# SwiGLU feed-forward on one core: the first 256 tokens turned on TensorE instead of in their load

## The chip, the cores and the metric

The kernel runs on one core of a Trainium2 chip. The metric is device microseconds of one execution. Durations of single instructions come from one profiled execution of each kernel.

## The reference

```python
B, S, D, F = 1, 2048, 512, 1376          # all bfloat16
def reference(x, w_gate, w_up, w_down):
    g = silu(x @ w_gate)                 # (2048, 1376)
    u = x @ w_up
    return (g * u) @ w_down              # (2048, 512)
```

## The kernel before

TensorE needs the contracted dimension on the 128 partitions. So the kernel holds x transposed: `xT_sb` has 128 partitions, four blocks of 128 features (`KD` = 4) and 2048 tokens. The tokens are worked in four chunks of 512 (`SC`), the 1376 columns of the two weights in ten blocks of 128 plus a rest of 96.

For a chunk `c` and a column block `ft` there are two groups of four matmuls: a gate group G and an up group U. Each group adds up over the four feature blocks into one of eight PSUM banks; the banks are taken in turn (`add_group`, group number modulo 8), and a group waits for the readers of the group eight places earlier. ScalarE takes silu of a G bank into `sg_sb` (L214), VectorE multiplies that with the U bank into `hT_sb` (L221). The rests of 96 columns are done in X groups (L283) and Y groups (L294). After all four chunks come sixteen O groups of eleven matmuls each (L311), which multiply `hT_sb` with w_down; VectorE copies their banks to `o_sb` (L225) and SyncE stores them (L197). The order on every engine is written out by hand; nothing is scheduled by a program.

The loads, on which the beginning depends, are issued from two queues.

- ScalarE's queue issues the first column block of w_gate and of w_up (`wg0`, `wu0`, 128 KB each), and only then loads its activation table and runs a small dummy activation (L203).
- SyncE's queue issues everything else, in this order: `x0a`, tokens 0 to 255, and `x0b`, tokens 256 to 511, by transposing loads (L73); then the weight slabs, always gate before up (L78): `wg1`, `wu1` (column block 1), `wg2`, `wu2` (blocks 2 and 3), `wg4`, `wu4` (4 to 6), `wg7`, `wu7` (7 to the end), the 32 last columns `wut`; then `x1`, `x2`, `x3` by transposing loads of 512 tokens each; then w_down.

TensorE first runs `N_WARM` = 10 matmuls on constants of one (L267), whose results nobody reads. Then the first pair of groups is worked in two halves of 256 tokens, so that it can begin when only `x0a` is there:

```python
for n0, n1 in ((0, HT), (HT, SC)):
    for g in groups[0:2]:
        gu_matmuls(g, n0, n1)
```

`gu_matmuls` waits once for each load that it is the first to need: `x0a` and `wg0`, then `wu0`, then `x0b` for the second halves, then `wg1`, `wu1`, `wg2`, `wu2` and so on. All later groups follow one after the other. GpSimd writes four small constants at the start (L334), and has nothing else to do.

Of the kernel before, what the change touches and what calls it, by code (L numbers as in the profile page):

```python
# [5 lines left out]
ALU = mybir.AluOpType  # L6
BF16 = mybir.dt.bfloat16
FP32 = mybir.dt.float32

N_WARM = 10  # L10


def bass_standalone__swiglu_ffn__prompt_kernel(nc, x, w_gate, w_up, w_down, out):
    _, S, D = x.shape
    F = w_gate.shape[1]
    P = 128
# [6 lines left out]
    TPC = SC // P  # L23
    NST = S // P
    LASTA = 384
    HT = SC // 2
# [5 lines left out]
    xf = x[0]  # L32
# [8 lines left out]
    with ExitStack() as es:  # L41
        sb = lambda name, shape, dt: es.enter_context(nc.sbuf_tensor(name, shape, dt))
        ps = lambda name, shape, dt: es.enter_context(nc.psum_tensor(name, shape, dt))
        sem = lambda name: es.enter_context(nc.semaphore(name))

        xT_sb = sb("xT_sb", [P, KD, S], BF16)
# [4 lines left out]
        sg_sb = [sb(f"sg_sb{i}", [P, SC], FP32) for i in range(NSG)]  # L51
        sgx_sb = [sb(f"sgx_sb{c}", [P, SC], FP32) for c in range(NSC)]
        sgy_sb = [sb(f"sgy_sb{c}", [P, SC], FP32) for c in range(NSC)]
        o_sb = [sb(f"o_sb{i}", [P, D], BF16) for i in range(NOS)]
        banks = [ps(f"bank{i}", [P, 512], FP32) for i in range(NB)]

        s_P = sem("s_P")
        s_A = sem("s_A")
        s_D = sem("s_D")
        s_out = [sem(f"s_out{i}") for i in range(NOS)]  # L60
        loads = {}

        def load_sem(name):
            loads[name] = sem(f"s_{name}")
            return loads[name]
# [6 lines left out]
        def load_x(eng, name, t0, t1):  # L72
            eng.dma_start_transpose(  # L73
                xT_sb[:, :, t0:t1], xf[t0:t1, :]
            ).then_inc(load_sem(name), 16)

        def load_w(eng, name, src, base, f0, f1):
            eng.dma_start(  # L78
                w_sb[:, :, base + f0:base + f1],
                src[:, f0:f1].rearrange("(k p) f -> p k f", p=P),  # L80
            ).then_inc(load_sem(name), 16)
# [1 line left out]
        slabs = [(0, 1), (1, 2), (2, 4), (4, 7), (7, NFT)]  # L83
        slab_of = {ft: a for a, b in slabs for ft in range(a, b)}

        def load_slab(eng, a, b):
            load_w(eng, f"wg{a}", w_gate, 0, a * P, min(b * P, F))
            load_w(eng, f"wu{a}", w_up, UPH, a * P, min(b * P, F - 32))

        def loads_on_scalar(act):  # L90
            load_slab(act, *slabs[0])

        def loads_on_sync(sp):
            load_x(sp, "x0a", 0, HT)
            load_x(sp, "x0b", HT, SC)
            for a, b in slabs[1:]:
                load_slab(sp, a, b)
            load_w(sp, "wut", w_up, F - (F - 32), F - 32, F)
            for c in range(1, NSC):
                load_x(sp, f"x{c}", c * SC, (c + 1) * SC)  # L100
            sp.dma_start(
                wd_sb[:, 0:NFF, :], w_down[0:NFF * P, :].rearrange("(k p) d -> p k d", p=P)
            ).then_inc(load_sem("wd"), 16)
            sp.dma_start(wd_sb[0:F_LAST, NFF, :], w_down[NFF * P:F, :]).then_inc(load_sem("wdt"), 16)
# [7 lines left out]
        def add_group(kind, **what):  # L112
            g = dict(kind=kind, at=len(groups), bank=banks[len(groups) % NB], readers=[], **what)
            groups.append(g)
            return g

        def add_op(eng, g, **what):
            n_read[eng] += 1
            op = dict(g=g, at=n_read[eng], **what)
            (act_ops if eng == "A" else dve_ops).append(op)  # L120
            g["readers"].append((eng, op["at"]))
            return op
# [37 lines left out]
        def plan_y(pi):  # L160
            g = add_group("Y", pi=pi)
            for c in (2 * pi, 2 * pi + 1):
                y0, y1 = yblk(c)
                d = add_op(
                    "D", g, kind="mul", out=hT_sb[0:64, NFF, c * SC:(c + 1) * SC],
                    a=sgy_sb[c][y0:y1, :], b=g["bank"][y0:y1, :], after=y_after[c],
                )
                t_ready[c] = d["at"]

        for c in range(NSC):  # L170
            for ft in range(NFF):
# [21 lines left out]
        def on_sync(sp):  # L193
            loads_on_sync(sp)
            for t, c0, c1, ob, eng, n in stores:
                sp.wait_ge(s_A if eng == "A" else s_D, n)
                sp.dma_start(of[t * P:(t + 1) * P, c0:c1], o_sb[ob][:, c0:c1]).then_inc(s_out[ob], 16)  # L197
            for i in range(NOS):
                sp.wait_ge(s_out[i], 16 * n_store[i])
# [28 lines left out]
        def on_tensor(pe):  # L228
            landed = set()

            def need(name):
                if name not in landed:
                    pe.wait_ge(loads[name], 16)
                    landed.add(name)

            read = {"A": 0, "D": 0}

            def after(eng, n):
                if n > read[eng]:
                    pe.wait_ge(s_A if eng == "A" else s_D, n)  # L240
                    read[eng] = n

            def free(g):
                if g["at"] >= NB:
                    for eng, n in groups[g["at"] - NB]["readers"]:
                        after(eng, n)

            def gu_matmuls(g, n0, n1):
                c, ft = g["c"], g["ft"]
                if c > 0:  # L250
                    need(f"x{c}")
                elif n0 < HT:
                    need("x0a")
                if c == 0 and n1 > HT:
                    need("x0b")
                need(("wg" if g["kind"] == "G" else "wu") + str(slab_of[ft]))
                col = (0 if g["kind"] == "G" else UPH) + ft * P
                for dk in range(KD):
                    ins = pe.matmul(  # L259
                        g["bank"][:, n0:n1], lhsT=w_sb[:, dk, col:col + P],  # L260
                        rhs=xT_sb[:, dk, c * SC + n0:c * SC + n1], start=(dk == 0), stop=(dk == KD - 1),
                    )
                if n1 == SC:
                    ins.then_inc(s_P, 1)

            for i in range(N_WARM):
                pe.matmul(banks[NB - 1][:, :], lhsT=ones_w, rhs=ones_m, start=True, stop=True)  # L267

            for n0, n1 in ((0, HT), (HT, SC)):
                for g in groups[0:2]:  # L270
                    gu_matmuls(g, n0, n1)

            for g in groups[2:]:
                free(g)
                kind = g["kind"]
                if kind in "GU":
                    gu_matmuls(g, 0, SC)
                elif kind == "X":
                    c = g["c"]
                    need(f"wg{slab_of[NFF]}")  # L280
                    need("wut")
                    for dk in range(KD):
                        ins = pe.matmul(  # L283
                            g["bank"][:, :], lhsT=w_sb[:, dk, XC0:XC0 + P],
                            rhs=xT_sb[:, dk, c * SC:(c + 1) * SC],
                            start=(dk == 0), stop=(dk == KD - 1),
                        )
                    ins.then_inc(s_P, 1)
                elif kind == "Y":
                    need(f"wu{slab_of[NFF]}")  # L290
                    for dk in range(KD):
                        for c in (2 * g["pi"], 2 * g["pi"] + 1):
                            y0, y1 = yblk(c)
                            ins = pe.matmul(  # L294
                                g["bank"][y0:y1, :], lhsT=w_sb[:, dk, YC0:YC0 + 64],
                                rhs=xT_sb[:, dk, c * SC:(c + 1) * SC],
                                start=(dk == 0), stop=(dk == KD - 1),
                                tile_position=(0, y0), skip_group_check=True,
                            )
                    ins.then_inc(s_P, 1)  # L300
                else:
                    t, c0, c1 = g["t"], g["c0"], g["c1"]
                    c = t // TPC
                    need("wd")
                    after("D", h_ready[c])
                    for fk in range(NFT):
                        K = P if fk < NFF else F_LAST
                        if fk == NFF:
                            need("wdt")
                            after("D", t_ready[c])  # L310
                        ins = pe.matmul(  # L311
                            g["bank"][:, 0:c1 - c0], lhsT=hT_sb[0:K, fk, t * P:(t + 1) * P],
                            rhs=wd_sb[0:K, fk, c0:c1], start=(fk == 0), stop=(fk == NFT - 1),
                        )
                    ins.then_inc(s_P, 1)

        on_sync(nc.sync)
        on_scalar(nc.scalar)
        on_tensor(nc.tensor)
# [29 lines left out]
```

## Time and profile before

| | |
|---|---|
| time, median of 3 runs | 121.25 us (121.11 to 121.77) |
| the profiled execution's own time | 121.6 us |
| its span, first to last instruction | 120.3 us |
| PE busy | 116.4 us, 97% of the span |
| VectorE, ScalarE, GpSimd busy | 43.7, 30.3 and 0.2 us |
| granted TensorE clock | 1.000 |

The span is the time from the first to the last instruction; 1.3 us of the profiled execution lie around it. PE stands for TensorE's matmuls, PEld for its weight loads, which run beside them. SPq and ACTq are the queues on which SyncE and ScalarE issue transfers. Times with two decimals in the views count from the start of the span.

### The profile page before, as it was taken

What the parts mean: (1) busy time and instruction counts of PE and PEld (TensorE: products, weight loads), DVE (VectorE), ACT (ScalarE), POOL (GpSimd) and SP (SyncE); (2) the same over time, 40 slices, a digit from 0 to 9 for tenths busy, and PEclk for the clock granted to TensorE, in tenths of its full rate; (3) what the DMA queues carried; (4) which work ended last, traced back from release to release, by engine and by line L of the source; (5) the groups of instructions that cost most, each with busy time, mean ns of one, the idle gap of its engine ahead of it and who ended that gap; (6) DMA issues with size and microseconds to landing.
All of it is one profiled execution on the core that took longest, in us unless ns stands there. A gap on an engine that the chain in (4) does not pass through costs nothing.

```text
span 120.3 us, 1386 instructions
## 1 busy us (share of the span) xinstructions
PE 116.4 (97%) x547; PEld 53.4 (44%) x557; DVE 43.7 (36%) x64; ACT 30.3 (25%) x51; POOL 0.2 (0%) x4
## 2 busy tenths in 40 slices
PE   7899999999999999999999999999999999999993
PEld 2354444444444444444444444444444444444452
DVE  0024434444334444334444334466233223222420
ACT  4032333262333272333262332330000000000001
POOL 0000000000000000000000000000000000000000
DMA  3999999970000000000000000000211121112112
GB/s 83 224 281 373 241 253 138 260 257 0 0 0 0 0 0 5 0 0 3 3 0 0 0 5 0 0 0 0 87 44 44 48 87 45 44 63 67 44 44 87
DMA packets 18022, 8.51 MB, mean 71 GB/s; under 512 B 11520, under 2 KB 18016, under 8 KB 18016
## 3 DMA queue, kind: packets, MB, share of 16 engines
q1 hardware_dynamic: 16960, 8.16, 26.7%
q10 hardware_dynamic: 1056, 0.26, 1.0%
q8 instruction: 4, 0.07, 0.2%
q14 instruction: 2, 0.02, 0.1%
HBM read 4.23 MB, written 2.10 MB: 53 GB/s over the span
## 4 chain that ended last, share of the span: by engine, by line
PE 90%; DMA 4%; SPq 3%; issue 1%; DVE 0%
PE bank L259 54%; PE bank L311 32%; DMA w_sb<-in_w_gate_dram 4%; PE bank L283 3%; SPq L73 2%; PE bank L294 2%; SPq L78 1%; DVE o_sb L225 0%
## 5 line engine op out<-in xcount | busy, mean ns | idle before, releaser
L259 PE MATMUL bank<-xT_sb,w_sb 128*128 128x512 bf16 (+1 forms) x322 | 69.4, 374 | 0.9 <-DMA xT_sb<-in_x_dram 0.4
L259 PEld LDWEIGHTS bank<-xT_sb,w_sb 128*128 128x128 bf16 x328 | 31.9, 98 | 38.2 <-DMA xT_sb<-in_x_dram 0.9
L221 DVE TENSOR_TENSOR hT_sb<-sg_sb,bank 128x512 bf16<-128x512 f32 x40 | 27.5, 688 | 46.0 <-PE bank L259 38.1
L311 PE MATMUL bank<-wd_sb,hT_sb 128*128 128x512 bf16 (+4 forms) x184 | 38.1, 367 | 0.2
L214 ACT ACTIVATE sg_sb<-bank 128x512 f32<-128x512 f32 x40 | 23.8, 596 | 43.4 <-PE bank L259 43.4
L311 PEld LDWEIGHTS bank<-wd_sb,hT_sb 128*128 128x128 bf16 (+1 forms) x187 | 17.8, 98 | 20.7 <-DVE hT_sb L221 0.4
L225 DVE CAST o_sb<-bank 128x512 bf16<-128x512 f32 (+1 forms) x16 | 10.7, 667 | 25.4 <-PE bank L311 25.3
L214 ACT ACTIVATE o_sb<-bank 128x384 bf16<-128x384 f32 x1 | 0.5, 490 | 38.2 <-PE bank L311 38.2
L267 PE MATMUL bank<-const-bfloat16-1.0 128*128 128x512 bf16 x10 | 4.0, 582 | 0.8 <-PEq L334 0.8
L283 PE MATMUL bank<-xT_sb,w_sb 128*128 128x512 bf16 x15 | 4.1, 380 | 0.1
L221 DVE TENSOR_TENSOR hT_sb<-sgx_sb,bank 32x512 bf16<-32x512 f32 x4 | 2.8, 692 | 3.5 <-ACT sgx_sb L214 3.5
L214 ACT ACTIVATE sgx_sb<-bank 32x512 f32<-32x512 f32 x4 | 2.3, 587 | 4.5 <-PE bank L283 4.5
L221 DVE TENSOR_TENSOR hT_sb<-sgy_sb,bank 64x512 bf16<-64x512 f32 x4 | 2.7, 684 | 0.1
L267 PEld LDWEIGHTS bank<-const-bfloat16-1.0 128*128 128x128 bf16 x10 | 1.3, 139 | 3.0 <-issue 3.0
L283 PEld LDWEIGHTS bank<-xT_sb,w_sb 128*128 128x128 bf16 x16 | 1.6, 98 | 1.9
L214 ACT ACTIVATE sgy_sb<-bank 64x512 f32<-64x512 f32 x4 | 2.4, 589 | 0.1
L294 PE MATMUL bank<-xT_sb,w_sb 128*64 128x512 bf16 x16 | 1.9, 383 | 0.0
L203 ACT ACT_TABLE_LOAD x1 | 1.3, 1283 | 1.7 <-issue 1.7
L294 PEld LDWEIGHTS bank<-xT_sb,w_sb 128*64 128x64 bf16 x16 | 0.8, 110 | 1.0 <-DVE hT_sb L221 0.4
L203 ACT ACTIVATE act_dummy<-const-float32-0.0 128x4 f32<-128x4 f32 x1 | 0.2, 206 | 0.0
L334 POOL MEMSET const-bfloat16-1.0<- 128x1 bf16 x1 | 0.1, 101 | 0.0
L334 POOL MEMSET const-uint8-127<- 128x1 uint8 x1 | 0.1, 101 | 0.0
(2 smaller groups left out, 0.2 us busy)
## 6 DMA issues: line engine op xcount, KB each, us to landing
out_dram<-o_sb SPq DMA_DIRECT2D x15, 128.0 KB, 1.7
wd_sb<-in_w_down_dram SPq DMA_DIRECT2D x1, 1280.0 KB, 6.7
w_sb<-in_w_gate_dram SPq DMA_DIRECT2D x1, 480.0 KB, 6.5
w_sb<-in_w_up_dram SPq DMA_DIRECT2D x1, 448.0 KB, 6.9
w_sb<-in_w_gate_dram SPq DMA_DIRECT2D x1, 384.0 KB, 5.2
w_sb<-in_w_up_dram SPq DMA_DIRECT2D x1, 384.0 KB, 5.7
w_sb<-in_w_gate_dram SPq DMA_DIRECT2D x1, 256.0 KB, 4.4
w_sb<-in_w_up_dram SPq DMA_DIRECT2D x1, 256.0 KB, 4.7
```

The lines of the kernel that those rows point to most:

```text
L73: eng.dma_start_transpose(xT_sb[:, :, t0:t1], xf[t0:t1, :]).then_inc(load_sem(name), 16)
L78: eng.dma_start(w_sb[:, :, base + f0:base + f1], src[:, f0:f1].rearrange("(k p) f -> p k f", p=P),).then_inc(load_sem(name), 16)
L203: act.activation(adummy[:, 0:4], zero_c, ACT.Silu)
L214: act.activation(op["out"], op["src"], fn).then_inc(s_A, 1)
L221: ins = dve.tensor_tensor(op["out"], op["a"], op["b"], ALU.mult)
L225: ins = dve.tensor_copy(op["out"], op["src"])
L259: ins = pe.matmul(g["bank"][:, n0:n1], lhsT=w_sb[:, dk, col:col + P], rhs=xT_sb[:, dk, c * SC + n0:c * SC + n1], start=(dk == 0), stop=(dk ...
L267: pe.matmul(banks[NB - 1][:, :], lhsT=ones_w, rhs=ones_m, start=True, stop=True)
L283: ins = pe.matmul(g["bank"][:, :], lhsT=w_sb[:, dk, XC0:XC0 + P], rhs=xT_sb[:, dk, c * SC:(c + 1) * SC], start=(dk == 0), stop=(dk == KD - 1),
L294: ins = pe.matmul(g["bank"][y0:y1, :], lhsT=w_sb[:, dk, YC0:YC0 + 64], rhs=xT_sb[:, dk, c * SC:(c + 1) * SC], start=(dk == 0), stop=(dk == ...
L311: ins = pe.matmul(g["bank"][:, 0:c1 - c0], lhsT=hT_sb[0:K, fk, t * P:(t + 1) * P], rhs=wd_sb[0:K, fk, c0:c1], start=(fk == 0), stop=(fk == ...
L334: nc = _bacc.Bacc("TRN2", target_bir_lowering=False, num_devices=1)
```

## The change

Tokens 0 to 255 are no longer brought by a transposing load. Two plain loads `t0` and `t1` bring 128 tokens each, with the tokens on the partitions, into a new tile `x0_sb`. GpSimd writes a 128x128 identity `ident`. TensorE multiplies each of the eight 128x128 blocks with it, which turns the block; the results stand in four new groups T (two blocks each) in banks 0 to 3. ScalarE copies the first and third of them, VectorE the second and fourth, to the places in `xT_sb` that `x0a` filled. The first G group waits in front of its first matmul for ScalarE's copies and in front of its third for VectorE's. The dummies go from ten to six. `x0b` and all other loads stay, in the same order, and all groups from G on move on by four banks.

```diff
-N_WARM = 10
+N_WARM = 6
...
+        x0_sb = sb("x0_sb", [P, TPC // 2, D], BF16)
+        ident = sb("ident", [P, P], BF16)
...
+        s_I = sem("s_I")
...
         def loads_on_sync(sp):
-            load_x(sp, "x0a", 0, HT)
+            for t in range(TPC // 2):
+                sp.dma_start(x0_sb[:, t, :], xf[t * P:(t + 1) * P, :]).then_inc(load_sem(f"t{t}"), 16)
             load_x(sp, "x0b", HT, SC)
...
+        x0_ready = []
+        for t in range(TPC // 2):
+            for half, eng in enumerate("AD"):
+                g = add_group("T", t=t, k0=2 * half)
+                op = add_op(
+                    eng, g, kind="copy", stored=(s_I, 0),
+                    out=xT_sb[:, 2 * half:2 * half + 2, t * P:(t + 1) * P],
+                    src=g["bank"][:, 0:2 * P].rearrange("p (k t) -> p k t", k=2),
+                )
+                x0_ready.append((2 * half, eng, op["at"]))
+        n_T = len(groups)
...
-                elif n0 < HT:
-                    need("x0a")
-                if c == 0 and n1 > HT:
+                elif n1 > HT:
                     need("x0b")
...
                 for dk in range(KD):
+                    if c == 0 and n0 < HT:
+                        for k0, eng, n in x0_ready:
+                            if k0 <= dk:
+                                after(eng, n)
...
+            pe.wait_ge(s_I, 1)
+            for g in groups[:n_T]:
+                need(f"t{g['t']}")
+                for i in range(2):
+                    k = g["k0"] + i
+                    ins = pe.matmul(
+                        g["bank"][:, i * P:(i + 1) * P], lhsT=x0_sb[:, g["t"], k * P:(k + 1) * P],
+                        rhs=ident[:, :], start=True, stop=True,
+                    )
+                ins.then_inc(s_P, 1)
...
+        nc.gpsimd.affine_select(
+            ident[:, :], ones_w, pattern=[[-1, P]], compare_op=ALU.is_equal, fill=0.0, base=0,
+            channel_multiplier=1,
+        ).then_inc(s_I, 1)
         on_sync(nc.sync)
```

Compiled, the changed program has one more instruction that the diff does not show: on GpSimd, directly ahead of the select, stands one that reloads the engine's library of routines by its index (index 0). GpSimd's program before holds no such instruction.

## The prediction

> **What bounds the kernel now.** I read the page first: which engine is full, and on which lines the last chain lies.
>
> ```profile
> span 120.3 us, 1386 instructions
> PE 116.4 (97%) x547; PEld 53.4 (44%) x557; DVE 43.7 (36%) x64; ACT 30.3 (25%) x51; POOL 0.2 (0%) x4
> PE bank L259 54%; PE bank L311 32%; DMA w_sb<-in_w_gate_dram 4%; PE bank L283 3%; SPq L73 2%; PE bank L294 2%; SPq L78 1%; DVE o_sb L225 0%
> ```
>
> TensorE is full. Only the 7% on DMA and SPq lie outside its work, so a change at the start moves the time by as much as it moves the last of the early waits. The chain of waits in order of time shows which one that is:
>
> ```profile
> 0.73 1.33 SPq L73
> ...
> 2.11 1.29 SPq L73
> ...
> 3.46 0.58 SPq L78
> ...
> 4.62 4.44 DMA w_sb<-in_w_gate_dram
> ...
> 9.11 3.41 PE bank L259 x15
> ```
>
> The chain does not go through x0a's landing. It goes through SyncE's issues, x0a and x0b at 1.3 us each, to the third slab's gate half, wg2, which is issued at 4.62 and lands at 9.06. From 9.11 on matmul follows matmul. The timeline shows the same start from TensorE's side (two windows; the short rows are single dummies):
>
> ```profile
> 0.77 4.02 PE L267 MATMUL bank<-const-bfloat16-1.0 128*128 128x512 bf16 x10 [0.77 <-PEq L334]
> 1.73 1.28 ACT L203 ACT_TABLE_LOAD   x1 [1.73 <-issue]
> 5.20 3.65 PE L259 MATMUL bank<-xT_sb,w_sb 128*128 128x256 bf16 x24 [0.41 <-DMA xT_sb<-in_x_dram]
> 9.11 13.99 PE L259 MATMUL bank<-xT_sb,w_sb 128*128 128x512 bf16 x63 [0.26 <-DMA w_sb<-in_w_gate_dram]
> 3.71 0.63 PE L267 MATMUL bank<-const-bfloat16-1.0 128*128 128x512 bf16 x1
> 4.41 0.38 PE L267 MATMUL bank<-const-bfloat16-1.0 128*128 128x512 bf16 x1
> ```
>
> Full-width matmuls follow each other at 13.99 / 64 = 0.22 us (one of 64 records is missing), the dummies at about 0.43: half speed. Only the last dummy is short (0.38), so full speed came near 4.3 us, 3.5 us after the first dummy; the granted clock says 1.00 all the time and does not show this. Between the first real matmul and wg2 lie 16 half-width and 8 full-width matmuls, 16 x 0.109 + 8 x 0.217 = 3.48 us. From 5.20 that ends at 8.68; wg2 lets it go on at 9.11. So the work runs as if it had begun at 9.11 - 3.48 = 5.63. This number is what the change must lower.
>
> **The change, part by part.** Transfers are priced by these rows of the page (size, then issue to landing):
>
> ```profile
> out_dram<-o_sb SPq DMA_DIRECT2D x15, 128.0 KB, 1.7
> w_sb<-in_w_gate_dram SPq DMA_DIRECT2D x1, 256.0 KB, 4.4
> w_sb<-in_w_gate_dram ACTq DMA_DIRECT2D x1, 128.0 KB, 2.6
> w_sb<-in_w_up_dram ACTq DMA_DIRECT2D x1, 128.0 KB, 3.7
> ```
>
> *SyncE's queue.* Removed: one transposing issue of 1.33 us. Added: two plain issues. A store of the same shape (128 rows of 1 KB) holds SyncE 0.33 us (L197's own view). So x0b is issued at 0.73 + 2 x 0.38 = 1.49 instead of 2.11, and every slab after it up to 0.62 us earlier.
>
> *The transfer engines.* They are full from 2 us on (busy share 1.24 in 2.9 to 4.8, 1.02 in 4.8 to 9.1), so earlier issue alone need not bring wg2 earlier; less work does. 256 KB in small pieces move at 251 GB/s (window 2 to 4), 1.04 us; in the larger pieces of window 10 to 12 at 379 GB/s, 0.69 us. That saves 0.35 us. wg2 therefore moves by 0 (if its own stragglers set it) to 0.62; I take 0.45, between the work saved and the issue gained: landing 8.61, work from 8.66.
>
> *t0 and t1.* Bounds by the rows above: 1.7 us with little beside it, 3.7 among other loads. t1, issued at 1.11, lands between 2.8 and 4.8; I take 2.6 us, the gate load on ACTq, which starts at the same moment: 3.7, and t0 0.4 earlier.
>
> *Six dummies.* They end near 0.77 + 6 x 0.42 = 3.3. The four that go were hidden in the wait for x0a; the turning matmuls take their place.
>
> *Eight turning matmuls* of width 128 are a quarter of a dummy, 0.107 us each at half speed, at most 0.14 with the dummies' weight load (139 ns): the first four from 3.3, t1's four from 3.7 to about 4.25.
>
> *The copies*, 128x256. VectorE: a cast of 128x128 takes 0.29 and of 128x512 0.69, so 0.42. ScalarE: 128x384 takes 0.49, so about 0.38; its table load ends at 3.01 and its dummy at 3.23, before the first copy is due. Behind these copies on both engines stand the first silu and the first product, which have nothing to work on before G0 anyway (before: ACT from 6.72). After the last turning matmul come its drain (about 0.16, a 512-wide matmul lasting 0.38 against 0.22 between starts), the copy and about 0.1 of semaphore: 4.25 + 0.16 + 0.42 + 0.1 = 4.9, in front of G0's third matmul. G0 so starts near 4.75 instead of 5.20. Without a stall it reaches wg2 at 8.23, ahead of 8.66: the new start is hidden behind wg2, with 0.4 us to spare. If wg2 does not move at all, nothing is gained.
>
> *x0b, wg1 and wu1* are due at 5.6, 6.5 and 7.4. Before they let their readers pass without a stall at 6.1, 6.9 and 7.8, and they now come 0.35 to 0.6 earlier: no cost. The banks shift by four; T's readers are done over 3 us before banks 0 to 3 are wanted again: no cost.
>
> *The identity.* TensorE waits for it after the dummies, and everything on TensorE is queued behind that wait. The select itself is small: a POOL row writing constants takes 0.10 us, VectorE's 128x128 row 0.29; from the barrier at 0.66 it would be there by 1.0. But ahead of it stands the library reload, which no row of before shows. Nearest rows: below, a POOL row, 0.10 (if it finds nothing to do); one load of tables into an engine, 1.28; above, the slowest transfer of the trace, 6.9 us from issue to landing (wu7). The identity is due at 3.3; each microsecond after about 4.1 is lost in full. I take the value below 3, by the rows of engines (0.10, 1.28) and not of bulk transfers, and keep the upper end for the range.
>
> A rule speaks against this. The Trainium skill, "GPSIMD Engine Reference", section 2.1, has the first call to a freshly loaded routine pay about 6 us for fetching its code. By that price the identity would come near 7 us and the time would be about 124.9. The page does not say whether an execution that finds the same library in place pays it, and no row here does.
>
> *Sum* against the profiled execution: 121.6 - 0.45 = 121.15. That execution lies 0.35 over the median; taken off, **120.8**, a gain of 0.4%. Its own bounds are 120.5 (wg2 earlier by 0.62, the start at its best) to 121.1 (0.1 to 0.2 gained).
>
> **A second rule, on the clock.** Row: full speed came 3.5 us after the first dummy of an unbroken row. Now the row is six dummies and eight small matmuls with gaps of a few tenths. "TensorE: Matmul & The Clock Gate", Part 1, states a busy window of about 3.4 us that starts at any phase; by it a gap could cost a whole further window, 0.6 us by the sum below.
>
> **Rivals.**
> - *Late identity (slower).* The reload takes over 3.4 us. With the identity at time I, G0 starts at I + 1.5 (1.0 for eight matmuls, 0.7 for drain, copy and semaphores, less 0.2), and as TensorE has been idle, its clock is slow until at most I + 3.5, which costs up to 1.0. For I = 4.9 (the middle between 1.3 and 6.9) the start is 6.4 to 7.4 instead of 5.63: 122.0 to 123.0. For I = 7.6 it is 9.1 to 10.1: 124.7 to 125.7. For it: the reload is there, and GpSimd did nothing like it before. Against: index 0 may be in place.
> - *Cold start (slower).* The gap behind the turning matmuls undoes the warm-up. Slow from 4.75 for 3.5 us: 1.75 of the 3.48 are done at 8.25, the rest at 9.98 against 9.11: +0.9, or +0.6 if the start is at its best: 121.9 to 122.1. For it: two gaps. Against: 0.41 us of idling at 4.79 in before did no harm, and 0.4 us of slack hides the first 0.8 of slow work.
> - *No change.* wg2 is held by its own transfer, not by what lies ahead: 121.1 to 121.4. For it: 4.4 us for 256 KB.
> - *Larger gain.* wg2 was late by chance in the profiled execution and the start decides: 5.20 to 4.6, with stalls gone: 120.2 to 120.5.
>
> **How the numbers follow.** Chances: forecast 0.38, late identity 0.36, cold start 0.10, no change 0.10, larger gain 0.06. A measurement of this kernel can tell about 0.5%, 0.6 us: faster means under 120.64, slower over 121.86. The forecast's 120.5 to 121.1 splits into 0.14 faster and 0.24 same. Faster 0.14 + 0.06 = 0.20; same 0.24 + 0.10 = 0.34; slower 0.36 + 0.10 = 0.46. The range leaves out 0.06 below 120.4 and about 0.13 above 125.3, the worst third of the late identity.
>
> **What would show it.** Right: the reload and select end before 3.3, the first L282 matmul starts at 4.6 to 5.0, its last early stall is still on wg2, and the long unbroken row starts near 8.65. Wrong: TensorE waiting for POOL; 128x256 matmuls at 0.21 us spacing instead of 0.11; wg2 still at 9.1.

## The result and the profile after

| | before | after |
|---|---|---|
| median of 17 runs each | 121.53 us (121.11 to 122.22) | 120.99 us (120.80 to 121.36) |
| ratio, 95% interval | 1 | 0.9955 [0.9938, 0.9973] |
| the profiled execution, its span | 121.6 us, 120.3 | 121.29 us, 120.0 |

The change gains 0.54 us on the medians, 0.45%; the forecast was 0.45 us. The page after, in the lines that answer to those of before (span, engines, the chain's shares):

```profile
span 120.0 us, 1415 instructions
PE 117.0 (97%) x561; PEld 53.9 (45%) x561; DVE 44.5 (37%) x66; ACT 31.1 (26%) x53; POOL 0.5 (0%) x5
...
PE bank L282 58%; PE bank L344 32%; PE bank L316 3%; PE bank L290 2%; PE bank L327 2%; PE bank L297 1%; ACT xT_sb L235 0%; DVE o_sb L246 0%
```

No transfer and no queue is on the chain any more. It runs through dummies, turning matmuls and one copy, and then only through matmuls, as the chain in order of time says:

```profile
0.84 2.72 PE bank L290 x6
3.56 0.80 PE bank L297 x6
4.36 0.02 issue
4.38 0.39 ACT xT_sb L235
4.77 0.14 issue
4.91 17.95 PE bank L282 x88
```

The timeline of the same stretch, with GpSimd and SyncE:

```profile
0.89 0.29 POOL L350 TENSOR_SCALAR_AFFINE_SELECT ident<-const-bfloat16-1.0 128x128 bf16<-128x128 bf16 x1 [0.38 <-POOLq L371]
...
1.73 1.30 SPq L76 DMA_TRANSPOSE xT_sb<-in_x_dram  x1
...
3.35 1.20 PE L297 MATMUL bank<-ident,x_sb 128*128 128x128 bf16 x8
...
4.25 0.51 SPq L81 DMA_DIRECT2D w_sb<-in_w_gate_dram  x1
...
4.91 9.31 PE L282 MATMUL bank<-xT_sb,w_sb 128*128 128x256 bf16 x48 [0.35 <-ACT xT_sb L235]
```

The identity is there at 1.18 us, two microseconds before it is wanted. wg2 is issued at 4.25 and, with the 3.9 us of its row, lands near 8.15. TensorE wants it at 8.66, when the weights for the next matmul are loaded, so it passes without a stall: the row from 4.91 is unbroken. What slows TensorE now shows in the groups kept apart by shape (last columns: busy, mean ns of one, idle before and its releaser). Before, the sixteen half-width matmuls (below, the halves) took 273 ns each; after:

```profile
L282 PE MATMUL bank<-xT_sb,w_sb 128*128 128x256 bf16 x16 | 2.4, 315 | 0.4 <-ACT xT_sb L235 0.4
```

The mean hides two kinds. The starts of the single matmuls lie 0.213 us apart up to 5.92 and 0.109 apart from 6.06 on: TensorE ran at half speed until near 5.97 us, 5.1 us after its first dummy. In the first trace of before that was 4.25 us, 3.5 after the first dummy. The granted clock reads 1.00 in both.

**A measure for all runs.** The third slab is that of `wg2`, column blocks 2 and 3. Nothing is late behind it, so I read the start of its first matmul (the 25th on `w_sb`) in every trace. The profiled execution's time is that moment plus 112.4 to 112.5 us in each of them: 9.11 and 121.6 before, 8.88 and 121.29 after, 11.28 and 123.72 in the slowest (`late_ident`). Without stalls and at full speed it comes 3.48 us after the first real matmul.

### The profile page after: what moved, and what is told of

It reads as the page before. It is cut to its first block, busy times and chain, and to the rows that moved or that the text cites. A ratio compares the mean times of both kernels' runs of the same rounds, so it can differ in the third digit from the quotient of the medians.

```text
span 120.0 us, 1415 instructions
## 1 busy us (share of the span) xinstructions
PE 117.0 (97%) x561; PEld 53.9 (45%) x561; DVE 44.5 (37%) x66; ACT 31.1 (26%) x53; POOL 0.5 (0%) x5
## 4 chain that ended last, share of the span: by engine, by line
PE 97%; ACT 0%; DVE 0%; issue 0%
PE bank L282 58%; PE bank L344 32%; PE bank L316 3%; PE bank L290 2%; PE bank L327 2%; PE bank L297 1%; ACT xT_sb L235 0%; DVE o_sb L246 0%
## 5 line engine op out<-in xcount | busy, mean ns | idle before, releaser
L282 PE MATMUL bank<-xT_sb,w_sb 128*128 128x512 bf16 (+1 forms) x328 | 70.2, 376 | 0.4 <-ACT xT_sb L235 0.4
L290 PE MATMUL bank<-const-bfloat16-1.0 128*128 128x512 bf16 x6 | 2.7, 623 | 0.8 <-PEq L371 0.8
L246 DVE CAST xT_sb<-bank 128x256 bf16<-128x256 f32 x2 | 0.8, 424 | 4.2 <-PE bank L297 4.0
L290 PEld LDWEIGHTS bank<-const-bfloat16-1.0 128*128 128x128 bf16 x6 | 0.7, 133 | 1.9 <-issue 1.9
L297 PE MATMUL bank<-ident,x_sb 128*128 128x128 bf16 x8 | 1.2, 309 | 0.0
L297 PEld LDWEIGHTS bank<-ident,x_sb 128*128 128x128 bf16 x8 | 0.8, 133 | 0.8 <-issue 0.5
```

The source lines that it names most:

```text
L246: ins = dve.tensor_copy(op["out"], op["src"])
L282: ins = pe.matmul(g["bank"][:, n0:n1], lhsT=w_sb[:, dk, col:col + P], rhs=xT_sb[:, dk, c * SC + n0:c * SC + n1], start=(dk == 0), stop=(dk ...
L297: ins = pe.matmul(g["bank"][:, i * P:(i + 1) * P], lhsT=x0_sb[:, g["t"], k * P:(k + 1) * P], rhs=ident[:, :], start=True, stop=True,)
```

## The experiments

The theory after the result: now the start binds (the turning chain, and the slow clock that the first matmuls meet), and the loads have time in hand, because the transposing load of x0a no longer stands ahead of them. Rivals: wg2 was early by chance in one execution; or the pauses around the turning matmuls keep the clock slow.

### The same two kernels again

> The changed kernel, unaltered. In its first trace the third slab's gate half (wg2) landed at 8.14 us, 0.5 before it was wanted at 8.66, and the first six half-width matmuls ran at half speed (spacing 0.21 us instead of 0.11). Start theory: the new kernel is bound by its own start (turning chain, 4.9 us) and the slow clock there; wg2 has time in hand in every execution, so the profile shows no stall on a load after the start, and the time is 121.0 us (ratio 0.995 to 0.997). If the clock turns at a moment that varies between executions, the slow matmuls end at another time than 6.0 us, anywhere from 3.5 to 7. Chance theory: wg2 was early by chance in one execution; here the profile shows a stall in front of wg2 again, near 8.7 to 9.1 us.

> The kernel before, unaltered, for another trace of its start. Transfer theory (wg2 is late in every execution, because x0a and x0b stand ahead of it): wg2 lands at 8.6 to 9.2, at or behind the moment when TensorE wants it (8.68), and TensorE stalls on it or arrives late through slow matmuls; third slab at 8.9 to 9.2. Chance theory: wg2 lands near 8.3 and no stall is seen.

> As before_a, one more execution: wg2 at 8.6 to 9.2 by the transfer theory, near 8.3 by the chance theory. By the free-moment theory of the clock the moment of full speed lies anywhere from 3.5 to 6.5 us, not at 4.25 as in the first trace.

`again`: median 121.07 us, ratio 0.9973 [0.9953, 0.9992], a gain of 0.39 us. Start at 4.77, third slab at 8.40, no stall on a load; wg2's row says 3.5 us after an issue at 4.24. The half-width matmuls now have a mean of 285 ns: full speed came near 5.2 us instead of 6.0, in the same program. Its time was 120.82.

`before_a` and `before_b`: 121.64 and 121.32 us; third slab at 9.17 and 8.84. Both stall, but on wu1, the slab half ahead of wg2. TensorE's weight loads, one line each:

```profile
8.29 0.55 PEld L259 LDWEIGHTS bank<-xT_sb,w_sb 128*128 128x128 bf16 x4 [0.59 <-DMA w_sb<-in_w_up_dram]
```
```profile
7.96 0.98 PEld L259 LDWEIGHTS bank<-xT_sb,w_sb 128*128 128x128 bf16 x6 [0.58 <-DMA w_sb<-in_w_up_dram]
```

So all three traces of before lose 0.27 to 0.43 us on a late slab (third slab less start less 3.48), not always the same one, and neither trace of after does. wg2 itself landed at 9.07, 8.99 and 8.61 before, at 8.14 and 7.72 after: 0.96 us earlier on average.

The chance theory still keeps a part. Which slab is late, and whether one is, differs between executions: `six_only` below has the loads of before unaltered, and in its trace wg2 landed at 8.33 and nothing waited for a slab. `gap_fill`, `turn_ten` and `late_ident` have the loads of the change unaltered; there wg2 landed at 8.19, 8.43 and 7.89. Over these four traces of the old loads and five of the new ones, wg2 lands 0.68 us earlier on average, and the four loads around it (x0b, wg1, wu1, wu2) 0.33 to 0.65. So the whole sequence has moved, by somewhat more than the 0.37 by which wg2 is issued earlier.

### The old load put back, for nothing

```diff
+            sp.dma_start_transpose(xs_sb[:, :, :], xf[0:HT, :]).then_inc(load_sem("xs"), 16)
             load_x(sp, "x0b", HT, SC)
...
```

> The changed kernel with the old transposing load of tokens 0 to 255 put back into SyncE's queue behind the two plain loads, into a tile that nobody reads. Transfer theory (the gain is that this load no longer stands ahead of x0b and the slabs): everything behind it is issued 1.35 us later and has 256 KB more ahead; wg2 lands at 9.1 to 9.5 again, TensorE stalls in front of it or before, at x0b (due 5.8, landing near 7) and wg1; time 121.6 to 122.2, ratio 1.001 to 1.006, at or above the kernel before. Start theory alone (the gain is the earlier start, the slabs have time in hand): time stays at 121.0, ratio 0.996.

Median 122.30 us, ratio 1.007 [1.0045, 1.0096]. The start is unchanged at 4.82; then TensorE does the first halves and stands:

```profile
4.82 1.25 PE L285 MATMUL bank<-xT_sb,w_sb 128*128 128x256 bf16 x8 [0.35 <-ACT xT_sb L238]
6.95 4.28 PE L285 MATMUL bank<-xT_sb,w_sb 128*128 128x256 bf16 x23 [0.87 <-DMA xT_sb<-in_x_dram]
```

x0b came at 6.9, issued at 3.08 instead of 1.73; the third slab at 9.56. With the early start kept and the transposing load back in the queue, the kernel is slower than before. This asks more than the old loads did: x0b is issued at 3.08 here and at 2.11 before, and t0 and t1 are moved as well. So it shows that later loads take the gain away, and not what the early start would be worth with exactly the loads of before.

### The loads of the change without its turning

Two forms. The first puts the plain loads straight into `xT_sb`; the tokens stay unturned.

```diff
-N_WARM = 10
+N_WARM = 6
...
-            load_x(sp, "x0a", 0, HT)
+            for t in range(2):
+                sp.dma_start(
+                    xT_sb[:, :, t * P:(t + 1) * P], xf[t * P:(t + 1) * P, :].rearrange("t (k f) -> t k f", f=P)
+                ).then_inc(load_sem(f"t{t}"), 16)
...
```

> The kernel before with two plain loads in place of x0a, put straight into xT_sb in pieces of 256 bytes, without turning them (so the first 256 tokens are left untransposed and their output rows are not the reference's), and with six dummies. It has the loads of the change without identity, turning matmuls and copies. Start theory: the real matmuls begin when t1 and wg0 have landed, near 3.9 to 4.1 us instead of 4.9, and then the next load is late: x0b (5.8) or wg2 (8.1), so that the work runs as if begun at 4.7 to 5.0; time 120.5 to 120.7, ratio 0.992. Chance theory: wg2 stays near 9.0 and decides: 121.2 to 121.4, ratio 0.998. Both: the turning chain costs no more than 0.5 us of the end.

Neither: 122.81 us in the median. Twelve runs fall into two bunches, three at 120.93 to 121.40 and nine at 122.41 to 123.57. The trace is of the second bunch:

```profile
0.77 2.72 PE L271 MATMUL bank<-const-bfloat16-1.0 128*128 128x512 bf16 x6 [0.77 <-PEq L338]
5.18 6.14 PE L263 MATMUL bank<-xT_sb,w_sb 128*128 128x256 bf16 x27 [1.70 <-DMA xT_sb<-in_x_dram]
```

In pieces of 256 bytes t1 landed at 5.1 us, not at 3.9 as in pieces of 1 KB. So TensorE idled for 1.7 us after six dummies, and then ran at half speed to 9.0 us: all sixteen halves have a mean of 415 ns. That cost 1.85 us (third slab at 10.51, less 5.18, less 3.48). The experiment missed its question and showed another thing, the cold start.

The second form keeps the pieces of 1 KB and the clock: loads into `x0_sb` as in the change, seven dummies, the tokens' place in `xT_sb` set to zero by GpSimd.

> The kernel before with the two plain loads of the change (1 KB pieces, into x0_sb) in place of x0a and with seven dummies; the first 256 tokens in xT_sb are set to zero by GpSimd instead, so no turning matmuls and no copies (the output rows of these tokens are not the reference's). TensorE still waits for t0 and t1. Start theory: G0 starts near 3.95, right behind the dummies; then x0b (5.5 to 5.8, due 4.8) or wg2 (7.7 to 8.2, due 7.5) is late, the third slab comes at 8.2 to 8.3 and the time is 120.6 to 120.75: the turning chain costs 0.1 to 0.3 us of the end, and loads take over right behind it. Rival (the turning chain is most of what is left): 119.9 to 120.2, third slab at 7.5.

120.97 us, ratio 0.9952 [0.9930, 0.9975], the same as the change. But not for the reason expected:

```profile
0.77 3.15 PE L271 MATMUL bank<-const-bfloat16-1.0 128*128 128x512 bf16 x7 [0.77 <-PEq L340]
3.94 7.31 PE L263 MATMUL bank<-xT_sb,w_sb 128*128 128x256 bf16 x36
```
```profile
L263 PE MATMUL bank<-xT_sb,w_sb 128*128 128x256 bf16 x16 | 3.0, 366 | 0.0
```

The start is 1.0 us earlier than with turning, and no load stalls it. It is given back on the clock: ten of the sixteen halves and most of the eleventh ran at half speed, until near 6.2 us (all sixteen have a mean of 366 ns). The third slab came at 8.49, where full speed from 3.94 would have given 7.42, or 8.07 by wg2, which landed at 8.02. A start before the clock is up counts half.

### Filling the pause

```diff
                 ins.then_inc(s_P, 1)
+            for i in range(2):
+                pe.matmul(banks[NB - 1][:, 0:HT], lhsT=ones_w, rhs=ones_m[:, 0:HT], start=True, stop=True)
```

> The changed kernel with two more dummies of half width (256 columns) behind the turning matmuls, where TensorE waits 0.56 us for the copies. Gap theory (the waits keep the clock slow): full speed comes near 4.4 us as in the kernel before, the first real matmuls follow each other at 0.11 us, and the time falls by 0.5 us against the changed kernel, to 120.5, ratio 0.991. Free moment theory (the clock turns at a moment that the gaps do not set): no gain on the median, 121.0, and the moment of full speed differs from that of the other traces without order.

Median 121.00 us, ratio 0.9969 [0.9950, 0.9989], against 121.07 for the unaltered change on the same chip: no gain. In its trace all halves run at full speed from 4.81 (mean 272 ns):

```profile
3.35 1.01 PE L297 MATMUL bank<-ident,x_sb 128*128 128x128 bf16 x8
4.20 0.38 PE L303 MATMUL bank<-const-bfloat16-1.0 128*128 128x256 bf16 x2
4.81 6.50 PE L282 MATMUL bank<-xT_sb,w_sb 128*128 128x256 bf16 x36 [0.23 <-ACT xT_sb L235]
```

But here the spacing of the turning matmuls falls from 0.107 to 0.056 us near 4.0, ahead of the two fillers, so they cannot be what brought full speed. The runs spread from 120.68 to 121.62, as those of the change do. So filling the short pause is worth nothing that 12 runs show. That the moment of full speed varies in the other executions of this kernel too is inferred from their times; one trace shows one moment.

### Six dummies alone, and ten with turning

```diff
-N_WARM = 10
+N_WARM = 6
```

> The kernel before with six dummies instead of ten and nothing else; x0a still lands near 5.2 us, so TensorE idles from 3.3 to 5.2. Bridge theory (the turning matmuls are what lets the change do with six dummies; the clock falls behind when TensorE idles 1.9 us in its first 5 us): in most executions the first real matmuls run at half speed for 1.5 to 3.5 us, the time rises to 122 to 123, ratio 1.005 to 1.015, with a spread of over 1 us between executions. Spare theory (the last four dummies were idle cover and the clock turns anyway 3.5 us after the first): 121.5, ratio 1.000.

Median 123.03 us. Again two bunches: four runs at 121.26 to 121.59, eight at 122.84 to 124.20. The trace is of the first: TensorE idles 1.89 us in front of x0a and still starts at full speed (mean 273).

```profile
0.77 2.72 PE L267 MATMUL bank<-const-bfloat16-1.0 128*128 128x512 bf16 x6 [0.77 <-PEq L334]
5.38 5.81 PE L259 MATMUL bank<-xT_sb,w_sb 128*128 128x256 bf16 x34 [1.89 <-DMA xT_sb<-in_x_dram]
```

Its row from 5.38 is unbroken: with the old loads, no slab was late in this execution, and the third slab came at 8.86. The second bunch lies 1.3 to 2.7 us over the median of before; in `no_turn` the slow clock cost 1.85. That the second bunch is the slow clock is inferred from `no_turn`, whose trace shows it; no trace of `six_only` caught it. With x0a's load, six dummies are too few. In the change they are enough: the turning matmuls begin right behind the dummies, at 3.35, and leave a pause of 0.35 us in place of 1.89.

The other way round, the change with ten dummies:

```diff
-N_WARM = 6
+N_WARM = 10
```

> The changed kernel with ten dummies instead of six. The dummies end near 4.9 instead of 3.35, so the turning matmuls wait for them and not for t1. Start theory: G0 starts near 5.9 (turning at the full clock in some executions) to 6.3 instead of 4.8, at full speed; the third slab is reached at 9.4 to 9.8 instead of 8.4 to 8.9: 121.8 to 122.2, ratio 1.003 to 1.006. Rival (the loads set the pace and the start has time in hand): 121.0, ratio 0.996.

122.34 us, ratio 1.0051 [1.0030, 1.0071], a little more than expected.

```profile
5.06 1.06 PE L297 MATMUL bank<-ident,x_sb 128*128 128x128 bf16 x8
6.47 4.75 PE L282 MATMUL bank<-xT_sb,w_sb 128*128 128x256 bf16 x29 [0.35 <-ACT xT_sb L235]
```

The turning begins at 5.1, still at half speed, and the start moves to 6.47; from there all runs at full speed (272 ns), third slab 9.98: the start is not covered by the loads.

### The identity made late

```diff
...
+        for i in range(3):
+            nc.gpsimd.affine_select(
+                scrap[:, i, :], nc.const_aps.tensor(1.0, [P, 1024], BF16), pattern=[[-1, 1024]], compare_op=ALU.is_equal,
+                fill=0.0, base=0, channel_multiplier=1,
+            )
         nc.gpsimd.affine_select(
```

> The changed kernel with three selects of 128x1024 into a tile that nobody reads ahead of the identity on GpSimd, to make the identity late on purpose. The 128x128 select took 0.29 us; the three take 3.8 us if half of that is a fixed cost and 7 us if all of it scales, so the identity comes at I = 5 to 8 us. The rival of the prediction had G0 start at I + 1.5 and the clock slow until I + 3.5 at most. By it the third slab is reached at I + 1.5 + 3.48 + 0 to 1.0, and as the time of the runs so far is 112.45 us more than that moment (120.82 for 8.40, 121.6 for 9.11, 122.99 for 10.51): 122.4 to 123.4 for I = 5, 125.4 to 126.4 for I = 8. If the wait for GpSimd were hidden by the loads, 121.0.

Four runs: 121.40, 123.61, 123.67, 123.72. GpSimd, TensorE and the halves of the slow kind:

```profile
0.89 3.02 POOL L352 TENSOR_SCALAR_AFFINE_SELECT scrap<-const-bfloat16-1.0 128x1024 bf16<-128x1024 bf16 x3 [0.38 <-POOLq L377]
3.86 0.29 POOL L356 TENSOR_SCALAR_AFFINE_SELECT ident<-const-bfloat16-1.0 128x128 bf16<-128x128 bf16 x1
```
```profile
4.21 1.03 PE L297 MATMUL bank<-ident,x_sb 128*128 128x128 bf16 x8 [0.65 <-POOL ident L356]
5.59 5.63 PE L282 MATMUL bank<-xT_sb,w_sb 128*128 128x256 bf16 x23 [0.35 <-ACT xT_sb L235]
```
```profile
L282 PE MATMUL bank<-xT_sb,w_sb 128*128 128x256 bf16 x16 | 3.6, 418 | 0.4 <-ACT xT_sb L235 0.4
```

The selects were faster than bounded, and the identity came at 4.15 us, the I of the rival. The start at I + 1.44 is as the prediction's rival had it. The clock is not: it stayed slow to 10.1 us, I + 6, and the third slab came at 11.28 instead of 9.1 to 10.1. By these rows TensorE idled 0.65 us in front of the identity and 0.35 in front of the copies, 1.0 together, and lost 2.2 us to the clock (11.28 - 5.59 - 3.48). One run of four, at 121.40, seems to have escaped; no trace of it was kept.

### Two attempts at a faster version

t1 first on ScalarE's queue, five dummies:

```diff
-N_WARM = 6
+N_WARM = 5
...
         def loads_on_scalar(act):
+            load_t(act, 1)
...
-            for t in range(TPC // 2):
-                sp.dma_start(x0_sb[:, t, :], xf[t * P:(t + 1) * P, :]).then_inc(load_sem(f"t{t}"), 16)
+            load_t(sp, 0)
```

> The changed kernel with t1 issued first on ScalarE's queue, beside t0 on SyncE's, and five dummies. t1 should land near 3.2 instead of 3.8 to 3.9 us, x0b and the slabs on SyncE's queue are issued 0.46 us earlier, wg0 and wu0 0.4 later (wu0 landing near 5.0 to 5.3). Start theory (the start binds): turning ends near 4.0, G0 starts near 4.5 instead of 4.8, 0.2 to 0.3 us less: 120.7 to 120.8, ratio 0.994. Rival (wu0 or the slow clock takes it back): the U0 matmuls wait for wu0, or more of the early work runs slow; 121.0, ratio 0.996 to 0.997.

122.82 us, ratio 1.0096 [1.0058, 1.0134]. t1 landed at 3.44, but t0 came later too (3.27 against 3.07) and wu0 fell from 4.9 to 5.9 behind the others. The start did not move (4.77), and the first U0 matmul waited for wu0 (0.54 us from the one ahead of it). More ran slowly, until near 6.9 us: the halves had a mean of 347 ns, and the third slab came at 9.43. The traced execution was the fastest of the seven, 121.83 us; why the others took up to 1.9 us more, no trace shows. With five dummies and a pause of 0.27 us behind them, the slow clock is the likely cause, as in `six_only`.

t0 and t1 as one load, with the filled pause:

```diff
-            for t in range(TPC // 2):
-                sp.dma_start(x0_sb[:, t, :], xf[t * P:(t + 1) * P, :]).then_inc(load_sem(f"t{t}"), 16)
+            sp.dma_start(
+                x0_sb[:, :, :], xf[0:HT, :].rearrange("(t p) d -> p t d", p=P)
+            ).then_inc(load_sem("t"), 16)
...
```

> The changed kernel with t0 and t1 as one load of 256 KB, issued once, and two half-width dummies behind the turning matmuls. The load should land near 3.5 (t0 3.0, t1 3.8 before), x0b and the slabs are issued 0.45 us earlier. Start theory: turning ends near 4.4 as before, G0 starts at 4.7 to 4.8 without a gap among the eight, 0 to 0.15 us less than the changed kernel: 120.85 to 121.05, ratio 0.995 to 0.997. Rival: with one issue the load lands at 3.9 as a whole, G0 starts at 5.1, 121.3.

121.05 us, ratio 0.9951 [0.9932, 0.9971], no different from the change. The load lands at 3.65 as a whole, so the turning begins 0.4 later and the start is 5.15, as the rival said; but all matmuls then run at full speed (272 ns), and the third slab comes at 8.66, between the 8.88 and 8.40 of the change's two traces. No version here beats the change.

## Why the prediction was right or wrong

**The sum was right, 0.45 us forecast and 0.54 measured, but it was reached by another way than the one forecast.** The loads moved more than forecast, the start did not hide behind them, and the slow clock took part of it back. That these nearly cancel is luck.

*The transfers: right in mechanism, too small.* Each plain issue held SyncE 0.40 us, not 0.33, so x0b and the slabs were issued 0.38 us earlier, not 0.62. Yet wg2 landed 0.96 us earlier on average over the five traces of the two kernels, and 0.68 over all nine with these loads, instead of 0.45. The term had 0.35 us for the work saved, from two bandwidths. I read one trace of before as if it stood for all; in four traces with the old loads a late slab cost 0.27 to 0.43 us in three and nothing in the fourth. Why the loads move by more than the issue is not shown, nor how much of it is chance in so few traces.

*The start hidden behind wg2: wrong.* This is the step that failed. With wg2 at 8.14 or 7.72, nothing hides the start; it binds. With ten dummies it came 1.63 us later than the mean of the change's two traces, and the time rose by 1.35; the rest fits the slow clock, 0.32 on average, that the later start no longer meets. The loads have little in hand, though. A start at 4.84 and full speed would reach wg2 at 8.32, and in `turn_ten` wg2 landed at 8.43; in `gap_fill`, which ran at full speed from 4.81, TensorE waited 0.05 us for wu1. With the clock up, loads and start would bind nearly together.

The start itself was well priced: 4.91 and 4.77 against 4.75, with copies of 0.42 and 0.38 us as predicted, and the turning matmuls at half speed. t1 came at 3.8 to 3.9 (3.7 predicted), but the reason given for its 2.6 us was misread: the gate load of 2.6 us is issued at 0.72, beside t0, and the load issued beside t1, wu0 at 1.17, took 3.7.

*The clock: wrong by assumption.* The prediction took full speed at 4.3 us from one trace. It came at 6.0 and 5.2 in two traces of the change, costing 0.49 and 0.15 us (third slab less start less 3.48). In `loads_only` it cost 1.07 us. Over nine traces without a long pause it came at 3.5 to 6.9 us (the list is at the end). A spread of 3.4 us fits what the Trainium skill, "TensorE: Matmul & The Clock Gate", Part 1, says of a window of about 3.4 us that starts at any phase. In one point the runs differ: `before_b` had full speed 2.8 us after its first dummy, sooner than a whole busy window takes. The rule was named in the prediction, but its price was not in the forecast's own range.

*What the gain is made of.* Three traces of before and two of the change give start -0.4 (mean of 5.20, 5.41, 5.09 to mean of 4.91, 4.77), stalls -0.33, clock +0.32: 0.4 us, beside 0.54 and 0.39 on the medians of the two comparisons. With so few traces the shares are rough.

*Late identity, chance 0.36: it did not come.* The reload is there in the trace, as two instructions of 11 ns:

```profile
L350 POOLq MODIFY_POOL_CONFIG  x2: 11/11/11, 0.8 to 0.8; - x2
L350 POOL TENSOR_SCALAR_AFFINE_SELECT ident<-const-bfloat16-1.0 x1: 292/292/292, 0.9 to 0.9; 128x128 bf16<-128x128 bf16 x1
```

The 6 us that the Trainium skill, "GPSIMD Engine Reference", section 2.1, has for a freshly loaded routine did not appear in any of the runs: the select starts 0.08 us after the first of the two. Whether a first execution pays it was not tried. The rival's arithmetic of the start held in `late_ident`; its bound on the clock was too kind by 2.5 us. Its I = 4.9 is called the middle between 1.3 and 6.9, which is 4.1; it comes out with the barrier's 0.66 and 0.1 for the select added.

*Cold start, chance 0.10: in part.* The first two to six real matmuls do run slowly in the change's traces. The full form, 122 us and more, did not come in 17 and 12 runs of the change, but 1.0 us of idling instead of 0.35 (by the rows of both) was enough to bring it in three runs of four (`late_ident`; one by its trace, two by their times). The price of 0.6 to 0.9 us was too low: the two traces that show it lost 1.85 and 2.2 us.

*Larger gain, chance 0.06: the nearest in mechanism.* It had the start decide, with the stalls gone, as came about; it left out the slow clock, and priced the start at 4.6 where 4.84 was measured.

## What to carry to other kernels

Where an early stall is taken away, ask what is late next with its own spread over executions: here one trace of before showed a stall on one slab, two more showed it on another, and a fourth with the same loads showed none. In these runs work that bridges a wait kept TensorE's clock as dummies do, and time gained in front of the moment of full speed counted half. Read the clock from the spacing of equal matmuls, not from the granted clock, and take more than one trace.

## What the runs showed of the hardware

- Where no row shows TensorE idle for over 0.41 us at once before full speed, half speed ended at 3.5 us (`before_b`), 4.0 (`gap_fill`), 4.25 (before), 4.7 (`one_load`), 5.2 (`again`), 5.3 (`scratch_x0a`), 6.0 (after), 6.2 (`loads_only`) and 6.9 (`split_queues`); `before_a` and `turn_ten` show only that it ended between 4.6 and 5.4 and between 5.8 and 6.5. The first dummy starts at 0.77 to 0.84 in all of them.
- Half speed ended at 9.0 and 10.1 us after idling of 1.7 and 1.0 us (`no_turn`; `late_ident`, in two pauses). A pause of 1.9 us did no harm in the trace of `six_only` and, by their times, in three more of its twelve runs.
- A 128 KB load of x in pieces of 1 KB landed 2.6 us after issue (t1 of the change), in pieces of 256 bytes 3.6 (t1 of `no_turn`).
- A select of 128x1024 on GpSimd took 1.0 us, of 128x128 0.29.
